# Three reorderings in a retention layer fused with a bilinear feed-forward: state copies after both products, one pair's transposing DMAs ahead of a store, one pair's products 24 matmuls later

## The chip, the cores and the metric

The kernel runs on one core of a Trainium2 chip. The metric is the device time of one execution in microseconds (us). A core has a matrix engine (TensorE, PE in the profile), a vector engine (VectorE, DVE), a scalar engine (ScalarE, ACT), a general engine (GpSimd, POOL) and SyncE (SP), which here issues nearly all DMAs. Each engine runs its own list of instructions in order and waits on semaphores for the others. Matmul results land in PSUM, which PE writes and DVE and ACT empty. All other tiles live in SBUF; inputs and the output are in HBM.

## The reference: what is computed

Two stages, float32 in and out; x never goes to HBM in the kernel.

```python
# q, k, v: 8 batches, 8 heads, 576 positions, 64 wide
scores = (q @ k.T) / sqrt(64)
gamma  = 1 - 2 ** (-5 - head)
ret    = (scores * (gamma ** (i - j) for i >= j else 0)) @ v
x = ret, heads side by side: 4608 tokens x 512
out = ((x @ w_a) * (x @ w_b)) @ w_out      # 512 -> 1536 -> 512
```

The decay gamma ** (i - j) splits into a factor of the query's position and one of the key's position. The kernel puts the first into a table that scales the attention's output (`qs`, `qs_o`) and the second into a table that scales the values (`vs`, `vs2`), so that between them a plain causal mask is left. Positions further back than a 64-row block reach a query through a running 64 x 64 state, the sum of (keys transposed times values) over the earlier blocks.

## The kernel before, in words

**The feed-forward sets the beat.** `ffn_block` (lines 687 to 759) goes over blocks of tokens: 512, 256, 256, and then 512 each. A block makes 12 products `pa` (x times w_a, line 705), copied by ACT to `ha` (line 713), and 12 products `pb` (line 720), which DVE multiplies by `ha` into `hT` (line 725). Then, for each 128 tokens, 12 matmuls make `po` (line 739), which ACT or DVE copies to `osb` (lines 754 and 756), and `store` (line 659) issues the DMAs to HBM on SP's queue. Each `pa`, `pb` and `po` takes one of the four PSUM buffers of `ps_ffn`, and `osb` has four SBUF buffers (`o_pool`, line 81), so the sixth `osb` waits until the second store has read its buffer. The block's generator yields a cost after each matmul, 1 for a width of 512 columns, and the running sum `at` is the clock of the program.

**The attention is slotted in.** Tokens come in pairs of 128 (256 tokens, the `n` of the code, 18 of them). Pairs 0 to 2 are handled in half-width steps (`STEPS`, line 160) with PE transposes. Pairs 0 and 1 are done before the feed-forward starts, all but one state; pair 2 (steps 4 and 5) is done inside block 0. From pair 3 (`FIRST`) on, a pair passes through these functions:

- `load_pair` (line 134) issues six DMAs on SP's queue, two each for q, k and v, into tiles of `stage`.
- `ahead` (line 434) casts q and k to bf16 (`qkb`, lines 441 and 445) and scales v (`vb`, line 446), seven POOL instructions.
- `turn` (line 467) issues two transposing DMAs on SP's queue (line 472), which read `qkb` and write `qkT`. Pair 3 alone is transposed by PE (`turned`).
- `stretch(into, outof)` (line 643) lets PE make the state increments `kv` of pair `into` (line 507) and its masked scores `sc` (line 564), and, for pair `outof`, the outputs `o` from the states (line 590) and from the scores (line 603). What ACT and DVE do with these (adds into `sums`, line 527; conversions into `states`, line 531; masks, line 573; scaling into x, line 613) is put into the list `later`, one entry of which is taken out after a product of the feed-forward (`pop`).

**The order of the work is written out by hand.** `todo` (lines 878 to 906) is a list of (place, function, arguments), sorted by place; entries of equal place stay in the order in which the list was built. Whenever `at` has reached a place, and the matmul just made closes an accumulation (or the fourth or eighth of a `po`), the functions due are called and their instructions go to the end of each engine's list. Block 0 ends at 144, block 1 at 216, block 2 at 288, block 3 at 432. In block 0 the matmuls of the second `po` allow calls at 112, 116 and 120; at 120 its copy and its store come first. In block 3 calls are possible every 8 before the first `po`, at 312, 320, 328, 336, 344, 352 and so on.

**The state of the second pair.** `first_totals` (line 867) runs at place 116. It makes, for the two halves of the heads (steps 1 and 3), the state after pair 1 in two PSUM banks of one tile `kv01`: `state_step` issues 16 matmuls (line 360), and one ACT copy into `left_states` (line 377) that reads the bank; then the same for the other half and the other bank.

**SP's queue.** It is one list. After the loads of the second half of the keys of pair 5 it holds: the two DMAs of the first store (line 667), the two of the second store, the two transposing DMAs of pair 4, two loads of v of pair 5, the third and fourth store, the transposing DMAs of pair 5, the loads of pair 6, and so on. Each DMA also waits until the DMA issued eight before it has landed.

Of the kernel before, what the change touches and what calls it, by code (L numbers as in the profile page):

```python
# [18 lines left out]
def kernel(  # L19
# [10 lines left out]
    nc = tc.nc  # L30
# [91 lines left out]
    def half(i):  # L122
        return slice(64 * i, 64 * i + 64)
# [37 lines left out]
    Q, K, V = 0, 1, 2  # L161
# [86 lines left out]
    left_states = const.tile([128, 2, 4, HP, 64], BF16)  # L248
# [93 lines left out]
            mask_s.rearrange("p k q s -> p (k q s)").unsqueeze(1)  # L342
            .to_broadcast([128, 4, 256]), op=ALU.mult)

    def state_step(i, behinds, kv=None):

        n, hh = STEPS[i]
        if kv is None:
            kv = ps_ffn.tile([128, 2, 2, 64], FP32, tag="ab", name="kv0")
        fresh = {0, 1}  # L350
        for behind in behinds:
            parts = [(n - 1, slice(0, 128))] if n % 2 else []
            parts.append((n, slice(0, 128) if behind else half(0)))
            for m, rows in parts:
                qkb, vb = natural[m, hh]
                for j in (0, 1):
                    for kp in (0, 1):
                        for r in (0, 1):
                            e0 = kp * 256 + (2 * j + r) * 64
                            nc.tensor.matmul(  # L360
                                kv[half(r), behind, j, :],
                                qkb[rows, 1, e0:e0 + 64],
                                vb[rows, e0:e0 + 64],
                                start=r in fresh, stop=True,
                                skip_group_check=True)
                            fresh.discard(r)
        cs = slice(2 * hh, 2 * hh + 2)
        into = {(0, 0): 0, (0, 1): 1, (1, 0): 2, (2, 0): 0}
        which = [b for b in behinds if (n, b) in into]
        if which:  # L370
            w = into[n, which[0]]
            for r in (0, 1):
                nc.scalar.copy(
                    state_after[half(r), w:w + len(which), cs, half(r)],
                    kv[half(r), which[0]:which[-1] + 1])
        if (n, behinds[-1]) == (1, 1):
            nc.scalar.copy(left_states[:, 0, 0, cs], kv[:, 1])
        elif (n, behinds[-1]) == (FIRST - 1, 1):
            if FIRST not in states_of:
                sums_of[1, 0] = sum_pool.tile([128, 4, HP, 64], FP32,  # L380
                                           tag="sums", name="sums")
                states_of[FIRST] = state_pool.tile(
                    [128, 4, HP, 64], BF16, tag="states", name="states")
            nc.vector.tensor_copy(sums_of[1, 0][:, 3, cs], kv[:, 1])
            nc.scalar.copy(states_of[FIRST][:, 0, cs], kv[:, 1])
# [402 lines left out]
    score_step(0)  # L788
    warm(3, 256)
    state_step(0, (0, 1))  # L790
    warm(1, 256)
    transpose_step(2, Q, "dve")
# [17 lines left out]
    warm(1, 256)  # L810
    cast_step(3, Q, "act")
    state_step(2, (0, 1))
    cast_step(3, K, "pool")
    warm(4, 256)
# [7 lines left out]
    load_w(W1, W2)  # L822
    score_step(3)
    state_step(1, (0,))
    warm(2, 256)
    state_step(3, (0,))
# [40 lines left out]
    def first_totals():  # L867

        kv = ps_o[0].tile([128, 2, 512], FP32, tag="o", name="kv01")
        for bank, i in ((0, 1), (1, 3)):  # L870
            state_step(i, (1,), kv[:, bank, 0:256].rearrange(
                "p (b j s) -> p b j s", b=2, j=2))

    def turn_step(i):
        transpose_step(i, Q, "act")
        transpose_step(i, K, "dve")

    todo = [(100, early_casts, ()), (112, turn_step, (4,)),
            (112.1, cast_step, (5, Q, "act")), (116, first_totals, ()),
            (116, score_step, (4,)), (116, state_step, (4, (0, 1))),  # L880
            (120, turn_step, (5,)), (128, output_step, (4,)),
            (128, score_step, (5,)), (128, state_step, (5, (0, 1))),
            (140, output_step, (5,))]
    todo += [(28 + 6 * step, pair_tables, (step,)) for step in range(13)]
    todo += [(170, stretch, (3, None)), (197, stretch, (4, 3)),
             (232, stretch, (5, 4)), (266, open_alone, (5,)),
             (270, close_outputs, (5,)), (312, stretch, (6, None)),
             (372, stretch, (7, 6)), (408, stretch, (8, 7))]
    for n in range(8, NP, 2):
        todo += [(starts[n] - 116, stretch, (n + 1, n)),  # L890
# [2 lines left out]
                 (starts[n] - 44, open_alone, (n + 1,))]  # L893
    todo += [(starts[NP - 2] - 40, close_outputs, (NP - 1,))]
    placed = {args[0]: at for at, fn, args in todo if fn is stretch}
    casts = {3: 117, 4: 117.1, 5: 141, 6: 200, 7: 250, 8: 330}
    turns = {4: 117.2, 5: 145, 6: 240, 7: 338, 8: 345}
    loads = {7: 212, 8: 271, 9: 345.1, 10: 345.2}
    todo += [(117.3, load_pair, (5, (V,))), (145.1, load_pair, (6, (K,))),
             (145.2, load_pair, (6, (Q,))), (145.3, load_pair, (6, (V,)))]  # L900
    for n in range(9, NP):
        casts[n], turns[n] = placed[n] - 70, placed[n] - 38
    todo += [(156 + 3 * part, turned, (3, part)) for part in range(4)]
    for fn, places in ((ahead, casts), (turn, turns), (load_pair, loads)):
        todo += [(at, fn, (n,)) for n, at in places.items()]
    todo.sort(key=lambda e: e[0])

    at = 0.0
# [40 lines left out]
```

## Time and profile before

| what | value |
|---|---|
| median of 5 runs | 330.56 us (330.54 to 332.3) |
| the profiled execution, its own time | 332.3 us |
| its span, first to last instruction | 330.6 us |
| PE busy | 323.2 us (98%) |
| DVE, ACT, POOL busy | 162.1, 128.9, 114.7 us |
| mean granted PE clock | 0.999 |
| HBM read, written | 37.75 MB, 9.44 MB |

The profiled execution lasts 332.3 us, of which 330.6 us lie between its first and its last instruction. It is the longest of the five runs that the median was taken from, 1.74 us above it. In the rows of the timeline, the first number is the start in us from the beginning of the span, the second the duration in us, then engine, line, operation, tiles, shapes and how many instructions were merged into the row; in brackets stands idle time of the engine before it and what ended it. Matmuls are pipelined: a row's duration is longer than the distance to the next row, so distances between starts are what counts on PE. SPq rows are issues of DMAs, not their transfers.

### The profile page before, as it was taken

Reading aid. Unit: us, or ns where it says so; the run is one execution under the profiler, and the core shown is the slowest. Engines: PE = TensorE matmul, PEld = TensorE weight load, DVE = VectorE, ACT = ScalarE, POOL = GpSimd, SP = SyncE. Lnnn points to the kernel's source line nnn. Section 1 sums busy time; section 2 is a strip of 40 time slices with the busy share of each in tenths; the row PEclk is TensorE's granted clock in tenths of the full one; section 3 lists DMA queues with packets and bytes.
Section 4 is the critical chain, followed back from the end, with each engine's and each line's share of the span. In section 5 each row is a group of like instructions: output and inputs, shape, how many; then the busy total and the mean of one; then the engine's idle time right before and its main releaser. Section 6 shows DMA issues by size and latency. Waiting matters only on the chain.

```text
span 330.6 us, 8740 instructions
## 1 busy us (share of the span) xinstructions
PE 323.2 (98%) x3660; PEld 169.5 (51%) x3660; DVE 162.1 (49%) x291; ACT 128.9 (39%) x277; POOL 114.7 (35%) x146
## 2 busy tenths in 40 slices
PE   7999999999989999999999999999999999999995
PEld 4764456858544554545454545454445444444443
DVE  5744435666544574756265626662456246414421
ACT  6834843563425334443235323532333333213321
POOL 3870068820957274653063405360420000000000
PEclk9999999999999999999999999999999999999999
DMA  7999999999899999990699158935850510031013
GB/s 209 253 184 208 255 228 223 192 210 208 195 207 258 208 209 234 209 217 34 163 204 230 43 137 183 222 88 139 177 113 4 144 48 0 2 95 34 1 31 96
DMA packets 143175, 50.37 MB, mean 152 GB/s; under 512 B 124576, under 2 KB 138656, under 8 KB 143136
## 3 DMA queue, kind: packets, MB, share of 16 engines
q1 hardware_dynamic: 138384, 45.10, 63.3%
q0 software_dynamic: 4752, 4.72, 8.8%
q8 instruction: 28, 0.46, 0.6%
q14 instruction: 11, 0.09, 0.1%
HBM read 37.75 MB, written 9.44 MB: 143 GB/s over the span
## 4 chain that ended last, share of the span: by engine, by line
PE 85%; DMA 6%; POOL 4%; issue 1%; SPq 1%; ACT 1%; DVE 0%; POOLq 0%; ACTq 0%
PE po L739 25%; PE pb L720 25%; PE pa L705 25%; DMA vf<-in_v_dram 3%; DMA qf<-in_q_dram 2%; POOL qkb L445 2%; POOL qkb L441 2%; DMA qkT<-qkb 2%; PE o L590 1%; PE o L603 1%; POOL vb L446 1%; PE kv L360 1%; PE sc L564 1%; PE kv L507 1%; PE pa L682 1%
## 5 line engine op out<-in xcount | busy, mean ns | idle before, releaser
L725 DVE TENSOR_TENSOR hT<-ha,pb 128x512 bf16<-128x512 bf16 (+1 forms) x120 | 75.7, 633 | 100.1 <-PE pb L720 94.6
L713 ACT CAST ha<-pa 128x512 bf16<-128x512 f32 (+1 forms) x120 | 64.8, 543 | 121.6 <-PE pa L705 117.3
L720 PE MATMUL pb<-xT,wb_sb 128*128 128x512 bf16 (+1 forms) x480 | 111.5, 358 | 0.1
L705 PE MATMUL pa<-xT,wa_sb 128*128 128x512 bf16 (+1 forms) x468 | 108.8, 357 | 0.0
L739 PE MATMUL po<-wo_sb,hT 128*128 128x512 bf16 (+1 forms) x444 | 97.5, 374 | 0.0
L720 PEld LDWEIGHTS <-wb_sb 128*128 128x128 bf16 x480 | 47.0, 98 | 46.5 <-issue 0.3
L705 PEld LDWEIGHTS <-wa_sb 128*128 128x128 bf16 x468 | 44.9, 98 | 44.2 <-issue 0.2
L739 PEld LDWEIGHTS <-hT 128*128 128x128 bf16 x444 | 42.3, 98 | 46.9 <-issue 0.2
L441 POOL CAST qkb<-qf 64x1024 bf16<-64x1024 f32 x15 | 15.5, 1031 | 81.8 <-DMA qf<-in_q_dram 70.5
L446 POOL TENSOR_TENSOR vb<-vf,vs 128x1024 bf16<-128x1024 f32 x15 | 28.5, 1902 | 14.7 <-DMA vf<-in_v_dram 7.9
L756 DVE COPY osb<-po 128x512 f32<-128x512 f32 (+1 forms) x16 | 10.8, 674 | 39.1 <-PE po L739 39.1
L754 ACT COPY osb<-po 128x512 f32<-128x512 f32 x20 | 11.7, 586 | 44.5 <-PE po L739 44.5
L613 DVE TENSOR_TENSOR xT<-o,qs 128x512 bf16<-128x512 f32 x30 | 19.5, 682 | 5.0 <-PE o L603 5.0
L527 DVE TENSOR_TENSOR sums<-kv,sums 128x256 f32<-128x256 f32 x46 | 19.5, 423 | 2.8 <-PE kv L507 0.8
L573 DVE TENSOR_TENSOR sT<-sc,mask 128x512 bf16<-128x512 f32 x30 | 19.5, 679 | 0.0
L445 POOL CAST qkb<-kf 64x512 bf16<-64x512 f32 x30 | 17.6, 615 | 0.9
L445 POOL CAST qkb<-qf 64x512 bf16<-64x512 f32 x30 | 17.6, 615 | 0.6
L441 POOL CAST qkb<-kf 64x1024 bf16<-64x1024 f32 x15 | 15.5, 1035 | 5.1 <-DMA kf<-in_k_dram 4.3
L531 ACT CAST states<-sums 64x512 bf16<-64x512 f32 x26 | 16.0, 617 | 0.3
L769 PE MATMUL w<-ones 128*128 128x256 bf16 (+1 forms) x36 | 8.2, 354 | 1.5 <-DVE ones L197 1.5
L299 POOL CAST qkb<-kf 128x512 bf16<-128x512 f32 x5 | 3.1, 616 | 19.0 <-DMA kf<-in_k_dram 19.0
L630 ACT COPY fence<-o 128x2 f32<-128x2 f32 x15 | 2.4, 161 | 16.6 <-PE o L590 16.6
(83 smaller groups left out, 163.7 us busy)
## 6 DMA issues: line engine op xcount, KB each, us to landing
qf<-in_q_dram SPq DMA_DIRECT2D x32, 256.0 KB, 4.8
kf<-in_k_dram SPq DMA_DIRECT2D x32, 256.0 KB, 5.1
vf<-in_v_dram SPq DMA_DIRECT2D x32, 256.0 KB, 5.1
out_dram<-osb SPq DMA_DIRECT2D x25, 256.0 KB, 2.2
out_dram<-osb SPq DMA_DIRECT2D x22, 128.0 KB, 2.4
wo_sb<-in_moe_w_out_dram POOLq DMA_DIRECT2D x3, 512.0 KB, 16.7
qf<-in_q_dram SPq DMA_DIRECT2D x8, 128.0 KB, 3.1
kf<-in_k_dram SPq DMA_DIRECT2D x8, 128.0 KB, 3.5
```

What stands on the lines that cost most here:

```text
L441: nc.gpsimd.tensor_copy(qkb[0:64, w], t[0:64])
L445: nc.gpsimd.tensor_copy(to[:, :, 1 - r], fro[:, :, r])
L446: nc.gpsimd.tensor_tensor(vb.rearrange("p (k h d) -> p k h d", k=2, h=H), vf.rearrange("p (k h d) -> p k h d", k=2, h=H), vs2[:, 2 if n in ...
L527: nc.vector.tensor_tensor(sums[:, i], own, prev, op=ALU.add)
L531: nc.scalar.copy(to(half(1 - r)), fro(half(r)))
L573: nc.vector.tensor_tensor(sT[:, on].rearrange("p c k s -> p (c k) s"), sc[:, on].rearrange("p c k s -> p (c k) s"), mask3.unsqueeze(1).to_ ...
L613: nc.vector.tensor_tensor(x_of(t0, 128).rearrange("p c (a s) -> p c a s", a=2), o[:, :, :, kp].rearrange("p a c s -> p c a s"), qs[:, :, s ...
L705: nc.tensor.matmul(pa[:, 0:n], wa_sb[:, c, fs], xT[:, c], start=(c == 0), stop=(c == NC - 1))
L713: nc.scalar.copy(ha[:, 0:n], pa[:, 0:n])
L720: nc.tensor.matmul(pb[:, 0:n], wb_sb[:, c, fs], xT[:, c], start=(c == 0), stop=(c == NC - 1))
L725: nc.vector.tensor_tensor(hT[:, F, 0:n], has[F][:, 0:n], pb[:, 0:n], op=ALU.mult)
L739: nc.tensor.matmul(po[:, 0:width], hT[:, F, u * 128:(u + 1) * 128], wo_sb[:, F, cols], start=(F == 0), stop=(F == NF - 1))
```

## The change

Three things are edited. `first_totals` collects the two ACT copies into `left_states` in a list and calls them after both halves' matmuls, where each copy followed its own half's. The casts of pairs 3 and 4, the transposing DMAs of pair 4 and the loads of v of pair 5 go from place 117 and after to place 116, behind `first_totals`, `score_step` and `state_step` of the same place. They were called at 120, after the second `po`'s store; now they are called four matmuls earlier, before it. So on SP's queue the two transposing DMAs and the two loads stand ahead of the two DMAs of the second store. And `stretch(6, None)` goes from place 312 to 336 in block 3. No instruction is added or taken away on any engine, and POOL's list keeps its order.

```diff
-    def state_step(i, behinds, kv=None):
+    def state_step(i, behinds, kv=None, copies=None):
...
         if (n, behinds[-1]) == (1, 1):
-            nc.scalar.copy(left_states[:, 0, 0, cs], kv[:, 1])
+            copies.append(lambda: nc.scalar.copy(left_states[:, 0, 0, cs],
+                                                 kv[:, 1]))
...
         kv = ps_o[0].tile([128, 2, 512], FP32, tag="o", name="kv01")
+        copies = []
         for bank, i in ((0, 1), (1, 3)):
             state_step(i, (1,), kv[:, bank, 0:256].rearrange(
-                "p (b j s) -> p b j s", b=2, j=2))
+                "p (b j s) -> p b j s", b=2, j=2), copies)
+        for copy in copies:
+            copy()
...
-             (270, close_outputs, (5,)), (312, stretch, (6, None)),
+             (270, close_outputs, (5,)), (336, stretch, (6, None)),
...
-    casts = {3: 117, 4: 117.1, 5: 141, 6: 200, 7: 250, 8: 330}
-    turns = {4: 117.2, 5: 145, 6: 240, 7: 338, 8: 345}
+    casts = {3: 116, 4: 116, 5: 141, 6: 200, 7: 250, 8: 330}
+    turns = {4: 116, 5: 145, 6: 240, 7: 338, 8: 345}
...
-    todo += [(117.3, load_pair, (5, (V,))), (145.1, load_pair, (6, (K,))),
+    todo += [(145.1, load_pair, (6, (K,))),
              (145.2, load_pair, (6, (Q,))), (145.3, load_pair, (6, (V,)))]
...
     for fn, places in ((ahead, casts), (turn, turns), (load_pair, loads)):
         todo += [(at, fn, (n,)) for n, at in places.items()]
+    todo += [(116, load_pair, (5, (V,)))]
```

## The prediction

> **What bounds the kernel now.** I read the page's busy shares and slices first, then the waits of PE, then the timeline of PE around each of these waits, and last the timeline of SP's queue and the chain.
>
> ```profile
> PE 323.2 (98%) x3660; PEld 169.5 (51%) x3660; DVE 162.1 (49%) x291; ACT 128.9 (39%) x277; POOL 114.7 (35%) x146
> DMA  7999999999899999990699158935850510031013
> PE sc L564 <- DMA qkT<-qkb: 1.4, 1, 1.4
> PE kv L360 <- ACT left_states L377: 0.4, 1, 0.4
> ```
>
> PE is the bound, and from 18 us on the list of its waits holds only the last two lines (total, times, longest). Everywhere else a 512-wide matmul follows the last after 0.216 us (`pa` x4 in 0.86 us in the chain). So a change of order can gain only at those two waits, at waits too short for the list, and it loses wherever it makes PE wait anew. The slices show the second fact: the DMA engines are full until about 149 us (slice 18 of 8.27 us is the first empty one). In that stretch DMAs land late and in the pace of the queue, and PE's work on a pair can come too early. The rows at the two waits, and at a shorter one between them:
>
> ```profile
> 43.57 0.44 PE L360 MATMUL kv<-vb,qkb 128*64 128x64 bf16 x16
> 44.37 0.44 PE L360 MATMUL kv<-vb,qkb 128*64 128x64 bf16 x16 [0.36 <-ACT left_states L377]
> 60.98 0.44 PE L507 MATMUL kv<-vb,qkb 64*64 64x64 bf16 x32
> 61.26 0.44 PE L564 MATMUL sc<-qkT 64*64 64x64 bf16 x32
> 68.10 0.44 PE L507 MATMUL kv<-vb,qkb 64*64 64x64 bf16 x32
> 68.56 0.45 PE L564 MATMUL sc<-qkT 64*64 64x64 bf16 x32
> 96.62 0.45 PE L507 MATMUL kv<-vb,qkb 64*64 64x64 bf16 x32
> 98.44 0.45 PE L564 MATMUL sc<-qkT 64*64 64x64 bf16 x32 [1.37 <-DMA qkT<-qkb]
> 121.25 0.44 PE L507 MATMUL kv<-vb,qkb 64*64 64x64 bf16 x32
> 121.56 0.45 PE L564 MATMUL sc<-qkT 64*64 64x64 bf16 x32
> ```
>
> Compare starts. From `kv` to `sc` it takes 0.28 us for pair 3 (a stretch without outputs) and 0.31 us for pair 8 (with outputs): no wait. Pair 4 takes 0.46 us, pair 6 takes 1.82 us. The SP queue and the chain say what pairs 4 and 6 wait for:
>
> ```profile
> 59.93 3.02 SPq L667 DMA_DIRECT2D out_dram<-osb  x4
> 63.05 3.54 SPq L472 DMA_TRANSPOSE qkT<-qkb  x2
> 66.65 1.26 SPq L142 DMA_DIRECT2D vf<-in_v_dram  x2
> 67.28 3.75 DMA vf<-in_v_dram
> 93.37 5.03 DMA qkT<-qkb
> ```
>
> The second transposing DMA of pair 4 is issued at 65.3 us and lands 3.2 us later (its line's issue-to-landing time), at 68.5, just when `sc` of pair 4 starts. That of pair 6 is issued at 93.37 and lands at 98.40, 0.04 us before its `sc`.
>
> **Part 1, the copies.** No instruction goes; the wait of the second product for the first copy goes. The two products start 0.80 us apart, and 32 products of pair 3 take 0.28 us, so 16 need at most that: 0.80 - 0.28 = 0.52 us. The shown idle time, 0.36, is the lower end, since rows overlap. I take 0.52, by the distances. What is late next: ACT's copies (0.27 us each) now start after the second product, at about 44.37 - 0.52 + 0.44 = 44.3 us, and end at 44.85, before the 45.12 of now. ACT stands idle before both now (0.36 and 0.53 us), and its next work, `state_after` at 45.57, waits for PE. The bank's next user, the first output of pair 2, comes at 48.71. So the later first copy costs nothing.
>
> **Part 2, the queue.** Moved on SP's list: two transposing DMAs and two loads of v go ahead of two stores. Moved on POOL's list: nothing, 14 casts and scalings keep their order. The new place asks for POOL's casts of pair 4 earlier: they end at 57.54 + 1.18 = 58.72 us, and SP reaches the place after the first store, about 59.93 + 3.02/2 = 61.4, so they don't hold SP. The transposing DMAs go out some 1.5 us earlier (half of 3.02), the second at 63.8, and land at about 67.0 with the same 3.2 us. `sc` of pair 4 comes, after part 1, at 68.56 - 0.15 - 0.52 = 67.9. Margin 0.9 us, so its excess of 0.46 - 0.31 = 0.15 us goes, and part 1's gain isn't taken back here, as it would be with the landing at 68.5. Part 2 alone is worth 0.15; with part 1, 0.67 together. Its bounds are nothing (position without effect) and, together, 0.36 to 0.70.
>
> What pays: the second store is issued about 2.6 us behind its present place in the queue, behind four DMAs. Its reader is ACT's copy of the sixth `osb`, which takes over that buffer:
>
> ```profile
> 70.89 0.41 ACT L534 CAST states<-sums 128x256 bf16<-128x256 f32 x1
> 71.20 0.40 ACT L536 CAST states<-sums 128x256 bf16<-128x256 f32 x1
> 71.61 1.25 ACT L531 CAST states<-sums 64x512 bf16<-64x512 f32 x2
> 72.87 0.59 ACT L754 COPY osb<-po 128x512 f32<-128x512 f32 x1
> 73.35 0.38 ACT L713 CAST ha<-pa 128x256 bf16<-128x256 f32 x1
> ```
>
> The same group of DMAs (store, two transposes, two loads) now ends with v's landing at 67.28 + 3.75 = 71.03; with the store last, I take the store's landing there. The copy would start at 72.87 - 0.67 = 72.2: margin 1.2 us, cost nothing. If the cover goes, `ha` behind it and then PE wait, microsecond for microsecond at most. From the third store on the queue has sent out the same DMAs as before, so the transposes of pair 5 land as now: issue at 72.75 (70.71 plus 1.94 + 0.10), 3.2 us, so 75.95, against `sc` of pair 5 at 76.77 - 0.67 = 76.1. That margin is 0.15 us only; a queue later by up to half a microsecond would take 0.35 back.
>
> A rule speaks against part 2. The Trainium skill's page "DMA: Bandwidth & Descriptors", section "Two DMAs through the same engine are not ordered", says that transfers of one queue start in order, but nothing orders their completion over the 16 engines, so an earlier place promises no earlier landing. Here the trace has rows that land in order of issue (68.5 for the transpose, 71.03 for v behind it), and I go by these. By the rule taken at its worst part 2 gives nothing, pair 4's wait takes part 1 back, and the sum below would be 1.54 us.
>
> **Part 3, pair 6 later.** 64 matmuls move behind 24 products of 512 columns: 24 x 0.216 = 5.2 us. `kv` of pair 6 comes at 96.62 - 0.67 + 5.2 = 101.1, `sc` at 101.4, 3.0 us after the landing at 98.40. The excess of 1.82 - 0.28 = 1.54 us goes (1.37 by the idle time). Three entries of `later` (four additions, four conversions, two masks) move with it to 340, 344 and 348, and the next stretch at 372 comes 24 products after the last. They sit beside `ha` and `hT` as before; the stretch of pairs 7 and 6, which brings the scaling into x on top of the same work, leaves PE at its beat of 0.86 us from 113.97 on in PE's timeline, so I cost them at nothing; their cover gone would be a few tenths. No DMA moves here: the transposes of pair 7 and the casts of pair 8 keep their places and follow SP's and POOL's pace. What is late next: PE is 2.2 us earlier after that, and pair 7's `qkT`, issued from 103.90 with 3.6 us to land, is there at 107.5, against `sc` at 113.30 - 2.2 = 111.1. Pair 9's are issued at 126.08 in a row of 2.66 us, so by about 132 at 3.6 us, against 134.94 - 2.2 = 132.7, the tightest place. But SP waits there for an `osb` copy that PE sets, so it moves along.
>
> **The sum.** 0.52 + 0.15 + 1.54 = 2.21 us off the profiled execution's 332.3 (span 330.6 and 1.7 around it): 330.1. That execution is 1.74 us above the median. The sum carried over to the median is 330.56 - 2.21 = 328.35, -0.67%.
>
> **The rivals.** (a) *Pair 6's wait hardly exists in the other runs.* The three lowest runs lie within 0.02 us at 1.74 us below the profiled one, close to the size of the wait (1.54), and a queue only 1.6% faster over 98 us would end it. Against: nothing shows where the 1.74 us lie. Then parts 1 and 2 remain: 330.56 - 0.67 = 329.9, no difference that the 0.3% (1.0 us, about what a measurement can tell) would show. A wait half as long gives 329.1. (b) *Landing doesn't follow the queue's order*: 0.67 lost, 330.56 - 1.54 = 329.0. Against: the landings of 68.5 and 71.03. Part 2 would then not do what it says. (c) *Slower: the second store lands late, and ACT's copy at 72.2 waits, and PE behind it.* For: ACT's rows there are back to back, so nothing absorbs a delay. It outweighs the gain from a landing at 72.2 + 2.2 = 74.4 on, and shows as slower from 75.4, 4.4 us after the end of the group now; at 76.0 the time is 330.56 - 2.21 + 3.8 = 332.2. Against: issue to landing of stores of this size is 2.4 us on the page.
>
> **How the numbers follow.** All three gains 0.60, with its own range 327.8 to 329.4; (a) 0.26, 329.4 to 330.3; (b) 0.05; (c) and its like 0.09. Faster is the first and (b) without a tail: 0.64. Same is (a) and that tail: 0.27. Slower 0.09. The likeliest is 328.4. The range goes from 327.7 to 330.5: below, the bounds 0.70 (pair 4 at 0.46 - 0.28) and 1.54 and the 0.60 us that PE loses beside pair 5's additions, should these fall better (five 256-wide groups from 77.93 to 80.73, at 0.44 each elsewhere); above, a height that takes in (a) and leaves out (c).
>
> **What would show it.** Right: `kv` L360 rows 0.28 us apart and no wait for `left_states`; `kv` to `sc` 0.31 us or less at pair 4; no wait of PE for `qkT` at pair 6; ACT's L754 near 72.2 us without a wait for a DMA. Wrong: PE's list of waits shows a new line at pair 5 (about 76 us) or at pair 9 (133 us), ACT idle before L754, or the span falls by 2 us while the unprofiled median does not.

## The result, and the profile after

| | before | after |
|---|---|---|
| median of all runs | 331.01 us (80 runs, 330.25 to 334.47) | 330.26 us (43 runs, 329.78 to 331.83) |
| a tenth of the runs lie below | 330.53 us | 329.90 us |
| a tenth of the runs lie above | 332.18 us | 331.08 us |
| profiled execution, own time (span) | 332.3 us (330.6) | 330.17 us (328.4) |

The ratio is 0.9976, with a 95% interval of 0.9967 to 0.9984: 0.24% faster, 0.75 us by the medians, where 2.21 us were forecast (the ratio is not the quotient of the two medians). Medians in this document leave out the few runs that lie more than 1.5% above the fastest of the same kernel. The two profiled executions, however, lie 2.13 us apart, close to the forecast. So the first question is not what the change did, but what those two executions stand for. The lower tenth of the runs gained 0.63 us, the upper tenth 1.10 us.

The busy shares and the DMA slices of the page after:

```profile
PE 322.5 (98%) x3660; PEld 169.3 (52%) x3660; DVE 162.1 (49%) x291; ACT 128.9 (39%) x277; POOL 114.7 (35%) x146
DMA  7999999989999899991899067935850510031013
```

Nothing has changed in what bounds the kernel: PE is busy for 98% of the span, and the DMA engines are full over the same first 18 slices. PE's list of waits from 20 us on has one line left (total, times, longest):

```profile
PE sc L565 <- DMA qkT<-qkb: 0.4, 1, 0.4
```

Both waits of before are gone. What is left stands in another place, as PE's timeline of after shows (start, duration, engine, line, operation, tiles, shapes, instructions merged). One row of before that the reading of part 1 needs comes first:

```profile
44.75 0.42 PE L331 MATMUL sc<-qkT 64*64 64x128 bf16 x16
```

```profile
42.99 0.69 PE L360 MATMUL kv<-vb,qkb 128*64 128x64 bf16 x32
43.61 0.42 PE L331 MATMUL sc<-qkT 64*64 64x128 bf16 x16
...
59.85 0.45 PE L508 MATMUL kv<-vb,qkb 64*64 64x64 bf16 x32
60.13 0.44 PE L565 MATMUL sc<-qkT 64*64 64x64 bf16 x32
66.97 0.44 PE L508 MATMUL kv<-vb,qkb 64*64 64x64 bf16 x32
67.28 0.44 PE L565 MATMUL sc<-qkT 64*64 64x64 bf16 x32
...
75.38 0.42 PE L508 MATMUL kv<-vb,qkb 64*64 64x64 bf16 x27
76.23 0.45 PE L565 MATMUL sc<-qkT 64*64 64x64 bf16 x32 [0.43 <-DMA qkT<-qkb]
...
101.18 0.45 PE L508 MATMUL kv<-vb,qkb 64*64 64x64 bf16 x32
101.46 0.44 PE L565 MATMUL sc<-qkT 64*64 64x64 bf16 x32
119.08 0.44 PE L508 MATMUL kv<-vb,qkb 64*64 64x64 bf16 x32
119.39 0.45 PE L565 MATMUL sc<-qkT 64*64 64x64 bf16 x32
```

Read it from the top. The 32 products for `left_states` have merged into one row. From its start to the next scores (line 331) it takes 0.62 us, where before took 44.75 - 43.57 = 1.18: the wait between the two halves was worth 0.56 us. Pair 4 takes 0.31 us from `kv` to `sc`, as forecast. Pair 5 takes 0.85 us, where executions without a wait take 0.24 to 0.26 from a row of this kind: a new wait of 0.6 us. Pair 6 takes 0.28, no wait. Pair 8 comes at 119.39, against 121.56 before.

The account of the two executions, by the starts of `sc`, before against after: pair 3 at 61.26 and 60.13 (1.13 us apart), pair 4 at 68.56 and 67.28 (1.28), pair 5 at 76.77 and 76.23 (0.54), pair 8 at 121.56 and 119.39 (2.17). Of the first 1.13 us about 0.55 are the copies. The other 0.59 lie in front of the whole change: the first `pa` of the feed-forward (line 682 before, 683 after) starts at 17.96 us in the one and at 17.37 in the other, in code that the change leaves as it was. In the other kernels below this start lies anywhere from 17.5 to 18.8 us. Then pair 4 gives 0.15 and pair 5 takes back 0.74 (0.60 by the wait, 0.14 ahead of it), and pair 6 gives 1.63 with what follows. So the change itself is worth about 1.6 us between these two executions, and 0.6 us are chance.

The queue of SP after, in its issues (not their transfers):

```profile
59.41 1.47 SPq L668 DMA_DIRECT2D out_dram<-osb  x2
60.99 3.03 SPq L473 DMA_TRANSPOSE qkT<-qkb  x2
64.08 1.25 SPq L142 DMA_DIRECT2D vf<-in_v_dram  x2
65.43 5.97 SPq L668 DMA_DIRECT2D out_dram<-osb  x6
71.51 2.66 SPq L473 DMA_TRANSPOSE qkT<-qkb  x2
```

Pair 4's second transposing DMA goes out at 62.5 us, where before it was 65.3, and lands at 65.92, not 68.52. That is the move at work. Pair 5's second goes out at 72.9 and lands at 76.19, against 72.7 and 75.98 before: PE was 1.28 us earlier and the queue was not. ACT's copy of the sixth `osb`, which takes over the second store's buffer, shows no wait for a DMA:

```profile
70.46 1.25 ACT L532 CAST states<-sums 64x512 bf16<-64x512 f32 x2
71.72 0.59 ACT L755 COPY osb<-po 128x512 f32<-128x512 f32 x1
```

### The profile page after: what moved, and what is told of

Its sections match the earlier page's. It is cut to its first block, busy times and chain, and to the rows that moved or that the text cites. A ratio compares the mean times of both kernels' runs of the same rounds, so it can differ in the third digit from the quotient of the medians.

```text
span 328.4 us, 8738 instructions
## 1 busy us (share of the span) xinstructions
PE 322.5 (98%) x3660; PEld 169.3 (52%) x3660; DVE 162.1 (49%) x291; ACT 128.9 (39%) x277; POOL 114.7 (35%) x146
## 4 chain that ended last, share of the span: by engine, by line
PE 95%; DVE 2%; DMA 1%; SPq 1%; issue 0%; ACT 0%; DVEq 0%; ACTq 0%
PE po L740 28%; PE pb L721 28%; PE pa L706 27%; PE w L770 2%; PE o L591 2%; PE o L604 1%; PE sc L565 1%; PE kv L508 1%; PE tp L316 1%; PE kv L360 1%; DMA qkT<-qkb 1%; PE pa L683 1%; PE sc L331 1%; PE o L411 1%; DVE sums L528 0%
## 5 line engine op out<-in xcount | busy, mean ns | idle before, releaser
L726 DVE TENSOR_TENSOR hT<-ha,pb 128x512 bf16<-128x512 bf16 (+1 forms) x120 | 75.7, 633 | 99.1 <-PE pb L721 93.5
L299 POOL CAST qkb<-kf 128x512 bf16<-128x512 f32 x5 | 3.1, 615 | 18.8 <-DMA kf<-in_k_dram 18.8
```

The source lines that it names most:

```text
L726: nc.vector.tensor_tensor(hT[:, F, 0:n], has[F][:, 0:n], pb[:, 0:n], op=ALU.mult)
```

## The experiments

The theory after the result: **how late a transposing DMA lands differs between executions by more than the wait it causes, so the 1.5 us at pair 6 exist in some executions only.** The expectations call it V or the theory. Each names its own opponent; the main one is that the wait was there in every execution and that something else gave its gain back. Where a ratio to before is given, before ran in the same batch on the same chip.

### The kernel before, once more

Nothing is edited.

> The kernel before, unchanged. Theory V (the wait of PE for pair 6's transposed tile differs from execution to execution, and the profiled one had an unusually long one): the profile shows another length of this wait than 1.4 us, likely 0.3 to 1.0, and an execution whose span is shorter by the difference. Theory N (the wait is the same 1.4 us in every execution, and something new in the changed kernel takes its gain back): the wait is 1.3 to 1.5 us again. Ratio 1.000 in both.

Measured: 331.77 us (12 runs), beside 331.35 us of the 35 runs of before in the same batch; ratio 0.9999 (0.9974 to 1.0024). Those 35 runs have two heights, 19 at 331.52 us or less and 16 at 332.0 or more; the other batches of before show no such gap. The profiled execution lasts 333.31 us, the longest of its twelve, and its waits of PE and its rows at pairs 4 and 6 are:

```profile
PE sc L564 <- DMA qkT<-qkb: 2.3, 2, 1.6
PE kv L360 <- ACT left_states L377: 0.4, 1, 0.4
```

```profile
68.15 0.44 PE L507 MATMUL kv<-vb,qkb 64*64 64x64 bf16 x32
69.34 0.45 PE L564 MATMUL sc<-qkT 64*64 64x64 bf16 x32 [0.76 <-DMA qkT<-qkb]
...
97.40 0.45 PE L507 MATMUL kv<-vb,qkb 64*64 64x64 bf16 x32
99.44 0.45 PE L564 MATMUL sc<-qkT 64*64 64x64 bf16 x32 [1.59 <-DMA qkT<-qkb]
```

The same program waits for pair 4 here too, 1.19 - 0.31 = 0.88 us by the starts, where the first profile showed 0.15. The wait at pair 6 is longer than either theory had forecast, so by itself this run decides between none. The landings are 69.30 and 99.39 us, against 68.52 and 98.40: one kernel, and landings that differ by a microsecond.

### Each part alone

Part 1 alone (only `first_totals` and `state_step` as in the diff), part 2 alone, and part 3 alone:

```diff
-    turns = {4: 117.2, 5: 145, 6: 240, 7: 338, 8: 345}
+    turns = {4: 116, 5: 145, 6: 240, 7: 338, 8: 345}
...          (part 2, with the casts and the loads of v, as in the diff)
-             (270, close_outputs, (5,)), (312, stretch, (6, None)),
+             (270, close_outputs, (5,)), (336, stretch, (6, None)),
...          (part 3)
```

> Only the copies follow both products. Both theories: the second product starts 0.28 us after the first, 0.5 us gained there. Pair 4's scores then wait for a transposed tile that lands when it did, so 0.3 to 0.7 us of wait stand there and the gain at 75 us is about 0. Time: same, -0.3 to +0.2 us against before.

> Only pair 4's transposing DMAs and pair 5's v go ahead of the second store. Pair 4's scores follow its products after 0.31 us or less: 0.15 us gained. Pair 5's scores follow without a wait or with one below 0.2 us. Time -0.3 to +0.2 us against before.

> Only pair 6's stretch goes 24 products on. Theory V: no wait at pair 6, and a median 0.3 to 0.9 us below before (the typical size of the wait), less than the 1.5 us of the profiled wait. Theory N: no wait at pair 6, and a median 1.4 to 1.6 us below before, since parts 1 and 2, whose gain ends in the new wait at pair 5, are not there.

Measured against the same 35 runs of before (331.35 us): part 1 alone 331.09 us, ratio 1.0001 (0.9971 to 1.0032), and its profiled execution ran at a granted clock of 0.756 and took 417.77 us, so it says nothing on the waits; part 2 alone 332.54 us, 1.0024 (0.9998 to 1.0050); part 3 alone 331.56 us, 0.9994 (0.9972 to 1.0016). No part can be told from nothing. But the interval of part 3 ends 0.9 us below before: a gain of 1.54 us in the typical run is ruled out, and even the theory's own 0.3 to 0.9 did not show. Part 2 alone, forecast within 0.3 us of before, leans to the slow side. The two traces say why part 3 is so small. Pair 6 with part 2 alone, still at its old place:

```profile
96.61 0.45 PE L507 MATMUL kv<-vb,qkb 64*64 64x64 bf16 x32
96.88 0.44 PE L564 MATMUL sc<-qkT 64*64 64x64 bf16 x32
```

No wait: the second transposing DMA of pair 6 landed at 96.02 us. With part 3 alone it landed at 95.44, about a microsecond ahead of the old place, so the move had nothing to remove there. Part 3 moves none of the DMAs ahead of pair 6's; landing in time was luck, not its doing. Over the five executions with transposing DMAs the landing of pair 6 was at 98.40, 99.39, 96.02, 95.44 and 95.41 us: two in which the old place waits, three in which it would not. As a frequency this count says little: the two are the longest of the runs beside them, the profiles of parts 2 and 3 alone the shortest of their twelve. Part 2's other runs lie up to 3.6 us higher; where they wait was not seen.

An account of these five executions says more about the runs that nobody profiled. Take from each one's own time the start of the first `pa` and the waits by the starts of the rows (over 0.31 us from `kv` to `sc` at pair 4, 0.25 at pair 5, 0.28 at pair 6):

| execution | own time | first `pa` | copies | pair 4 | pair 5 | pair 6 | left |
|---|---|---|---|---|---|---|---|
| before | 332.30 | 17.96 | 0.56 | 0.15 | 0 | 1.54 | 312.09 |
| before, once more | 333.31 | 18.00 | 0.55 | 0.88 | 0.01 | 1.76 | 312.11 |
| part 2 alone | 330.74 | 17.86 | 0.56 | 0.01 | 0.01 | 0 | 312.30 |
| part 3 alone | 330.81 | 17.86 | 0.55 | 0.31 | 0.01 | 0 | 312.08 |
| after | 330.17 | 17.37 | 0 | 0 | 0.60 | 0 | 312.20 |

What is left is the same within 0.22 us. So by this account the 1.74 us that the first profile lay above its median are the wait at pair 6 for the most part, and not the scatter of the start. And an estimate follows: if no run starts its first `pa` before 17.37 us, the earliest in any profile here, a run of before that holds the whole 1.54 us lasts at least 312.08 + 17.37 + 0.56 + 1.54 = 331.55 us. Of the 80 runs of before, 58 are shorter. The whole wait is in 22 of them at most.

The changed kernel was not run again beside these, and parts 1 and 2 together were not run with transposing DMAs.

### Plain copies in place of the transposing DMAs

To set the landing by hand, the following kernels have two plain DMAs for each pair in place of the transposing ones. Queries and keys stay untransposed, so the attention is left out in part and these kernels are compared among themselves. The plain copies land earlier (pair 5 at 73.4 to 75.7 us, pair 6 at 91.5 to 94.2 without further loads); their 256-byte pieces go out as 2 KB packets.

```diff
-            nc.sync.dma_start_transpose(
-                qkT[:, w].rearrange("p k c s -> p (k c) s"), qkb[:, w])
+            nc.sync.dma_start(
+                qkT[:, w].rearrange("p k c s -> p (k c) s"),
+                qkb[:, w].rearrange("p (x s) -> p x s", s=128))
```

> The order of the kernel before, but with a plain DMA from SBUF to SBUF (1024 pieces of 256 bytes, as many as a transposing DMA moves) in the place of each transposing DMA. Queries and keys are left untransposed, so the attention is not what the reference has; the queue, the waits and all other work stay. This is the base for the next three, which are compared with it alone. Both theories: within 1 us of before, PE's wait for the left states at 44 us is there, and the second copy of pair 6 lands at 95 to 99.5 us, with a wait at pair 6 if that is after 96.9.

> The changed kernel's order with the same plain DMAs (the same part of the attention left out). Theory V (the wait at pair 6 is there in some executions only; in the others the gain is parts 1 and 2 less a wait at pair 5): 0.3 to 1.2 us below the base, no wait at pair 6, a wait of 0 to 1 us at pair 5, and a smaller upper tail. Theory N (1.5 us at pair 6 in every execution): 1.5 to 2.2 us below the base.

> Parts 1 and 2 with the same plain DMAs (the same part left out), pair 6 at its old place. Theory V: between the base and the changed order, 0 to 0.6 us above the changed order by the median, with the upper tail back. Rival W (part 3 is worth nothing): the same median and the same tail as the changed order. Theory N: 1.5 us above the changed order.

Measured: base 330.95 us, all three parts 330.47, parts 1 and 2 without part 3 330.61. With the landing in time, parts 1 and 2 give 0.34 us and part 3 another 0.14, both within the spread of twelve runs. None of the three profiles shows a wait at pair 5 or 6.

Part 1 alone and part 3 alone, in a second batch on another chip:

> Part 1 alone with the plain DMAs in whole pieces (the same part left out), against the base with them. No wait for left states at 44 us; the copies of pairs 4 and 5 land early enough to take nothing back, or 0.1 to 0.4 us at pair 4. Expected 0.2 to 0.55 us below the base's median.

> Part 3 alone with the plain DMAs in whole pieces (the same part left out), against the base with them, where the copy of pair 6 landed at 94.2 us, before it was wanted. Expected: the base's time within 0.3 us, since there is no wait to take away.

Measured: part 1 alone 330.39 us, part 3 alone 330.98. Part 3's profile still has the line `PE kv L360 <- ACT left_states L377: 0.4, 1, 0.4`, part 1's has not. They lie 0.59 us apart, as the 0.52 us of the copies would have it; the base itself did not run in this batch. Here nothing lands late behind part 1, and it keeps its gain.

Could pair 5 be moved on as pair 6 was, now that it waits? All three parts, and pair 5's stretch later:

```diff
-             (232, stretch, (5, 4)), (266, open_alone, (5,)),
+             (240, stretch, (5, 4)), (266, open_alone, (5,)),
```

> The changed order with pair 5's stretch 8 places (1.7 us) later, at 240 for 232, with the same plain DMAs (the same part left out). If pair 5's wait takes back what parts 1 and 2 win: no wait at pair 5, and 0.3 to 0.7 us below the changed order. If another wait behind it makes up for it, or the copies land earlier than the transposes did: the same time as the changed order.

Measured: 331.72 us, 1.25 us more than without the edit. PE's timeline of this kernel shows one reason:

```profile
85.91 0.21 PE L592 MATMUL o<-qkT,states 64*64 64x64 bf16 x1
86.54 0.44 PE L592 MATMUL o<-qkT,states 64*64 64x64 bf16 x31 [0.42 <-ACT states L533]
```

The outputs of pair 5 now wait 0.6 us for the states, which ACT makes from the products that were moved, and PE's list of waits has another 0.3 us for an ACT copy (`fence`) behind them. Pair 5 has work close behind it, which pair 6 has not.

### A late landing, first try

Pair 6's two copies were cut into pieces of 128 and 64 bytes, to make them slower, at the old place and at the new one.

```diff
+            s = (64, 32)[w] if n == 6 else 128
...
-                qkT[:, w].rearrange("p k c s -> p (k c) s"),
-                qkb[:, w].rearrange("p (x s) -> p x s", s=128))
+                qkT[:, w].rearrange("p k c (t s) -> p (k c t) s", s=s),
+                qkb[:, w].rearrange("p (x s) -> p x s", s=s))
```

> Parts 1 and 2 with plain DMAs as before (queries and keys untransposed), and the two DMAs of pair 6 in smaller pieces, 64 and 32 elements for 128, so that they carry the same bytes in 2 and 4 times as many pieces and land some 4 to 5 us later. Pair 6 at its old place. Expected: landing at 96 to 99.5 us, a wait of PE of 0.5 to 3.5 us at pair 6, and a time above the run with whole pieces by that much.

> The changed order with the same small pieces for pair 6 (and the same part of the attention left out). If part 3 takes away the wait when it is there: no wait at pair 6, the time of the changed order with whole pieces within 0.3 us, and below its partner at the old place by the partner's wait (0.5 to 3.5 us). If the late landing holds up something else (the stores, the next pair's loads): the two are alike.

A miss. The packets were of the same sizes as without the edit, the landings were at 91.5 and 93.7 us, and no profile had a wait. 330.54 and 330.38 us say nothing on a late landing, only once more that the two places cost the same without one.

### A late landing, second try

Four loads of 256 KB that nothing reads stand ahead of pair 6's two copies in the queue; parts 1 and 2 are in both kernels, and only the place of pair 6 differs. In a second pair three such loads stand ahead of pair 5's copies, without and with parts 1 and 2.

```diff
     def turn(n):
+        for i in range(4 if n == 6 else 0):
+            nc.sync.dma_start(
+                qs_o[:, i].rearrange("p (h d) -> p h d", h=H),
+                q[i, :, 0:128, :].rearrange("h s d -> s h d"))
         qkb = of(natural, n)[0]
```

> Plain copies stand in for the transposing DMAs (the attention's keys and queries stay untransposed, so the output is not the reference's), parts 1 and 2 of the change, pair 6 at its old place, and four loads of 256 KB that nothing reads, ahead of pair 6's two DMAs on SP's queue. The same without the four loads had its landing at 92.3 us against sc at 95.9. Four loads at about 1.2 us each make the landing about 97 us, an estimate. Theory (the 1.5 us wait is there in an execution exactly when the landing is late): kv to sc at pair 6 shows an excess of about 1 us, and the time lies that much over the next kernel's of this batch. Rival (pair 6's wait costs nothing, because the feed-forward catches up later, so that its 1.5 us never were in the median): the excess shows, but the two times agree within 0.3 us.

> As the kernel before it in this batch, with the same four loads, and pair 6 at its new place, 24 products on. Theory: no excess at pair 6 (landing about 97 us, sc about 101 us), and a time lower than the other's by about the excess that the other shows. Rival: the two times agree within 0.3 us.

Measured: at the old place 333.89 us, at the new place 330.50. The ratios to before are 1.0023 (0.9991 to 1.0054) and 0.9947 (0.9925 to 0.9968): the intervals are far apart. PE at the old place, then at the new one:

```profile
96.25 0.45 PE L513 MATMUL kv<-vb,qkb 64*64 64x64 bf16 x32
99.90 0.47 PE L570 MATMUL sc<-qkT 64*64 64x64 bf16 x32 [3.20 <-DMA qkT<-qkb]
100.31 1.89 PE L711 MATMUL pa<-xT,wa_sb 128*128 128x512 bf16 x4
101.99 1.82 PE L726 MATMUL pb<-xT,wb_sb 128*128 128x512 bf16 x4
103.65 1.03 PE L711 MATMUL pa<-xT,wa_sb 128*128 128x512 bf16 x4
104.51 1.03 PE L726 MATMUL pb<-xT,wb_sb 128*128 128x512 bf16 x4
```

```profile
101.09 0.44 PE L513 MATMUL kv<-vb,qkb 64*64 64x64 bf16 x32
101.36 0.44 PE L570 MATMUL sc<-qkT 64*64 64x64 bf16 x32
```

The landing at 99.86 us ends a wait of 3.65 - 0.28 = 3.4 us; at the new place the landing of 97.77 us is 3.6 us early. The two profiled executions last 335.58 and 329.89 us, 5.7 apart: 3.4 the wait, 1.6 a lower clock behind it (the last section), 0.3 the start of the first `pa`, and the rest not placed. That the medians differ by 3.4 us too is chance, since the profiled execution at the old place lies 1.7 us above its median; how long the others waited was not seen. The rival, that the feed-forward makes such a wait good, falls all the same: with a late landing part 3 is worth at least the wait, and without one (the comparisons above) it is worth nothing that can be measured.

> Plain copies in place of the transposing DMAs (the attention's keys and queries stay untransposed, so the output is not the reference's), otherwise the kernel before, with three loads of 256 KB that nothing reads ahead of pair 5's two DMAs on SP's queue. The same without the loads landed at about 75.7 us or earlier, so about 78 us here, an estimate, against sc of pair 5 at about 76.8 us: an excess of about 1 us at pair 5. Theory (a late landing at pair 5 takes back what parts 1 and 2 gave): the next kernel's excess is larger by 0.5 to 0.7 us and its time agrees with this one's within 0.3 us. Rival (parts 1 and 2 keep their gain): this one is slower than the next by 0.5 us or more.

> As the kernel before it in this batch, with the same three loads, and with parts 1 and 2 of the change. Theory: landing of pair 5 at the same 78 us, excess at pair 5 larger by 0.5 to 0.7 us than in the other, and the same time within 0.3 us. Rival: the landing comes earlier with the queue by as much as the products do, and the time is lower by 0.5 us or more.

Measured: 331.75 us without parts 1 and 2, 332.79 with them, in the same batch. PE at pair 5, without them and with them:

```profile
76.39 0.44 PE L512 MATMUL kv<-vb,qkb 64*64 64x64 bf16 x28
77.44 0.45 PE L569 MATMUL sc<-qkT 64*64 64x64 bf16 x32 [0.62 <-DMA qkT<-qkb]
```

```profile
76.17 0.42 PE L513 MATMUL kv<-vb,qkb 64*64 64x64 bf16 x27
78.58 0.45 PE L570 MATMUL sc<-qkT 64*64 64x64 bf16 x32 [1.99 <-DMA qkT<-qkb]
```

The products come 0.22 us earlier and the scores 1.14 us later, because the landing is at 78.54 us, not 77.40. The profiled executions differ by 1.05 us and the medians by 1.04. So the time goes by the landing, and what the products gained in front of it is lost: the theory's direction, and the rival, a kernel faster by 0.5 us or more, is wrong. But the theory had said the same time for both, and the kernel with parts 1 and 2 is slower. Either part 2's order makes the landing later, as the lean of part 2 alone (332.54 us) would have it, or it is chance: the runs with parts 1 and 2 reach from 331.41 to 334.72 us, the others from 331.27 to 334.40. No run isolates it.

## Why the prediction was wrong

**Part 1, the copies: right.** 0.52 us were forecast. The row of 32 products shows the wait gone, worth 0.56, and with plain copies part 1 alone lies 0.59 us below part 3 alone.

**Part 2, the queue: right in place, wrong in what comes next.** Pair 4's excess went. Its landing came 2.6 us earlier, 2.0 if the execution's earlier start is taken off, where the working had 1.5; the rival in which the landing does not follow the queue did not occur. ACT's copy was forecast at 72.2 us without a wait and came at 71.72 (in an execution that started 0.59 us earlier): no sign of the slower rival. But the margin of 0.15 us at pair 5 was not enough. The working said that a queue later by up to half a microsecond would take 0.35 us back; it took 0.60. It set PE's 76.1 us against a landing of 75.95; in the profile after PE was ready at 75.6 and the landing was at 76.19. The queue had kept its own time while PE came earlier, both by the change and by its earlier start.

**Part 3, pair 6 later: the step that failed.** "The excess of 1.82 - 0.28 = 1.54 us goes" is true of the profiled execution, and the profile after shows it gone. The failing step is the next one, in the sum: "carried over to the median". In the median run there is no wait of 1.54 us to remove. Part 3 alone gained nothing that could be measured, a gain of more than 0.9 us lies outside its interval, and by the account above at least 58 of the 80 runs of before are too short to hold the wait. Where pair 6's landing comes at 95.4 to 96.0 us, as in three profiles, it is ahead of the old place. The prediction had the warning in its own rows: the profiled execution was the longest of five, 1.74 us above the median, and three runs agreed within 0.02 us. It put that into rival (a), "Pair 6's wait hardly exists in the other runs", with a chance of 0.26. That rival comes nearest to what happened: it gave a gain of 0.67 us, and 0.75 were measured. Its row stood on firmer ground than the row that was preferred, since a profile shows what one execution waited for, and a run that much longer spent time somewhere that the others did not. Against it the prediction set "nothing shows where the 1.74 us lie", and rightly: such a surplus need not be the wait that the profile shows most plainly. The base with plain copies was profiled in an execution 1.55 us above its median without any wait at pair 6; it waited 1.0 us for a load of weights.

**What the 0.75 us are made of** is settled only in part. All runs shifted by about 0.6 us, the slowest tenth by half a microsecond more. The shift agrees with parts 1 and 2, the loss of the tail with part 3; neither is shown. Nor need the gain be the same elsewhere: in four batches of the experiments before's own median was 331.35, 332.08, 331.48 and 332.84 us, and the changed kernel ran in none of them. How often pair 5 takes parts 1 and 2 back was seen in one execution only, the one after.

**The range** of 327.7 to 330.5 us took in 330.26, thanks to rival (a). The sign shown first by "what would make it wrong" came true twice: a new wait at pair 5 at about 76 us, and a span that falls by 2.2 us while the median falls by 0.75.

## What to carry to other kernels

Before a wait that a profile shows is put into a sum, compare that execution's own time with the median; if it lies above by about the size of the wait, the wait may be that execution's alone. Then take the start and the waits from that time: what is left says which of the other runs are too short to hold the wait. A wait for a DMA out of a full queue belongs to the landing, not to the instruction: moving the consumer later paid here when the landing was late and not otherwise, and moving work ahead of it paid nothing while the landing stayed. Two edits that make an engine earlier should be checked at the next place where that engine meets the queue, and a margin there smaller than the scatter of landings (here 0.15 us against about 1) should be counted as lost.

## What the runs showed of the hardware

**The same DMA lands up to 4 us apart.** Pair 6's second transposing DMA landed between 95.41 and 99.39 us in five executions that issue the same DMAs ahead of it up to small moves. Nor need a landing be late as a whole: the trace has sixteen signals of completion for each DMA, and in the first profile of before fifteen of them stand at 96.63 to 96.91 us, when PE was ready, and only the last at 98.40. In the second profile of before all sixteen stand at 99.19 to 99.39. In the traces the instruction fetches of 16 KB (one packet, 0.9 to 1.7 us) also fall at different times, 95.8 to 98.3 us near this place; whether they hold the others up was not shown, and the cause of the scatter stays open.

**A long wait costs twice.** In the kernel with the late landing at the old place, the windows around the wait read (window, length, busy time of the five engines with counts, granted clock, DMA share, GB/s):

```profile
96.00:98.00 2.00, 0.70 (x34) 0.33 (x32) 1.50 (x4) 0.09 (x1) 0.00 (x0) 1.00 1.12 324
98.00:100.00 2.00, 0.10 (x12) 0.10 (x16) 0.80 (x2) 0.00 (x0) 0.00 (x0) 1.00 1.07 195
100.00:102.00 2.00, 2.00 (x37) 0.82 (x38) 0.00 (x0) 0.00 (x0) 0.44 (x1) 0.54 0.81 184
102.00:104.00 2.00, 2.00 (x7) 0.77 (x6) 0.08 (x1) 1.73 (x4) 1.90 (x4) 0.60 1.05 234
104.00:106.00 2.00, 2.00 (x11) 0.88 (x9) 2.00 (x4) 1.34 (x3) 1.94 (x3) 1.00 1.16 319
```

After the 3.20 us of idle PE the granted clock is 0.54 and 0.60 on average over two windows, 0.50 between 100.20 and 103.55 us, and the two groups of four matmuls after `sc` take 1.68 and 1.66 us from start to start in place of 0.86. That is 1.6 us on top of the wait. It is common in that kernel: eight of its twelve runs have a mean granted clock of 0.995 or less, as the profiled one has, and last 333.66 to 336.86 us; the other four have 0.999 or 1.000 and last 330.76 to 333.67. The waits of 1.4 to 2.0 us in the other profiles brought no such drop. The Trainium skill's page "TensorE: Matmul & The Clock Gate", section "Part 1: The HAM clock gate", says that the array falls to half its clock after an idle window of about 3.4 us and needs a busy one of the same length to come back. The slow stretch here, 100.31 to 103.65 us, agrees with the second; the idle time was a little below the first, and why it was enough is not shown.

**Small pieces were joined.** Plain copies from SBUF to SBUF in 256-byte pieces that follow on from each other left as 2 KB packets (28,672 packets of 256 bytes fewer in the trace, 3,584 of 2 KB more), and cutting the pieces to 128 and 64 bytes changed nothing.
